# Moving splits, evictions, squares and last outputs of a two-level feed-forward kernel

## The chip, the cores and the metric

One core of a Trainium2 chip runs the whole program. The metric is the device time of one execution in microseconds (us). The times shown for the kernel before are 1060.23, 1060.93 and 1061.2 us, with 1060.93 as their median.

The engines are named as in the profile: PE is TensorE (PEld its weight loads), DVE is VectorE, ACT is ScalarE, POOL is GpSimd, SP is SyncE, which here only issues DMAs.

## The reference

Causal attention with a cumulative bias runs over 4 batches, 8 heads and 576 positions. Its output, seen as 2304 tokens by 512, passes through two feed-forward blocks. The second of these is where nearly all of the change lies:

```python
def _moe_ref(x, w_in, w_out) -> np.ndarray:
    h = x @ w_in
    g = np.maximum(h, 0.0) + np.log1p(np.exp(-np.abs(h)))
    return (g @ w_out).astype(np.float32)
...
def _moe2_ref(x, w_gate, w_val, w_out, rms_g) -> np.ndarray:
    rms = np.sqrt(np.mean(x * x, axis=-1, keepdims=True) + 1e-06)
    xn = x / rms * rms_g
    g = xn @ w_gate
    silu = g * (1.0 / (1.0 + np.exp(-g)))
    val = xn @ w_val
    return (silu * val @ w_out).astype(np.float32)
```

The first block has 2048 hidden columns, the second 1536 for the gate and 1536 for the value.

## The kernel before

Every fp32 operand of a matmul is held as a high half (a copy rounded to fp32r, made on ACT) and a low half (the operand minus its high half, made on DVE or POOL). A product is three matmuls: high by high, high by low, low by high.

The program has three stages: attention, the first feed-forward (96 steps over six token tiles of 384), and the second feed-forward. The second one walks three **groups** of 768 tokens, and within a group 12 **steps**, one for each 128 hidden columns. Steps are numbered n = 0 to 35, a group change stands at n = 12 and n = 24. `m2_g(n)` writes one step. It forms gate and value of a 2 by 2 block product with seven block products instead of eight. Each block product is `prod`, six matmuls with 384 columns. In the order of the code they are, with the PSUM bank they write:

- P1: weight A12 by activation form B21 into D, P2: A11 by B11 into A
- O0: `m2_out(n-1, 0)`, nine matmuls with 512 columns: the output of the step before, token tiles m = 0, 1, 2
- P3: S2 by T2 into A
- O1: `m2_out(n-1, 1)`, nine matmuls, token tiles m = 3, 4, 5
- P4: S1 by T1 into D, P5: S3 by T3 into A, P6: S4 by B22 into D, P7: A22 by T4 into A

There are two banks, D and A, so each product waits until the one before it in its bank has been read: P3 for `c1` (ACT copies A, L1011), P5 for `u2` (ACT, L1030), P6 for `m5` (ACT, L1038), P7 for `vB` (DVE adds A and m5, L1047), P4 for `gA` (DVE, L1015), the next P1 for `gB` (DVE, L1049), the next P2 for L1052 (DVE). A sigmoid on ACT (L1016) stands between gA and `s0`. `m2_hi` (ACT, L985) and `m2_lo` (DVE, L990) split the gated values for the outputs. Half 0 of a step is split at its end, half 1 (the `l` tile of L1057) in the step after.

The order on each engine is the order of the code: nothing reorders it (`manual_schedule`), and a list of due times only decides which function is called before which. Each engine works through its own list in that order.

Beside the products, each step splits the weights of the next one (`u_split`, four pieces: ACT high L924, POOL low L925) and loads those of the step after it (`u_load`, SP). At a group change the activation forms are new: `n_split` splits seven forms for two column blocks j = 0, 1 (ACT high L968, low L970 on DVE or POOL by an even or odd index). In step 11 or 23 (`ahead`) these are B21, B11 and T2; in step 12 or 24 (`fresh`) T1 and T3 after O0, B22 after u2, T4 after m5. Also `m2_evac` copies the finished group's six output tiles from PSUM in two halves each and stores them: m = 0, 1, 2 in step 12 after P4, m = 3, 4, 5 in step 13 ahead of O0. Odd m go over ACT (L1082), even ones over DVE (L1084). Since O0 and O1 of step 13 write the same banks anew, they wait for these copies.

`m1_ss` squares the last tile of the first feed-forward (ACT, L863) and adds the square to a sum (POOL, L865), four times, with one tile for the square. By the due times three of these stand between steps 0 and 1, the fourth after step 1. `m2_end` writes the last outputs: O1 of step 34, then the six tiles of step 35 in the order m = 0 to 5, with copies on ACT and DVE and twelve stores on SP.

Of the kernel before, what the change touches and what calls it, by code (L numbers as in the profile page):

```python
# [14 lines left out]
AF = mybir.ActivationFunctionType  # L15
# [130 lines left out]
def attention_moe_kernel(ctx, tc, q, k, v, s, w_in, w_out, w_gate, w_val, w_out2, rms_g, out):  # L146
# [710 lines left out]
    def m1_ss(t, a):  # L857
        y = st["yt", t, a]
        if a == 0:
            st["acc", t] = ss_tile("acc")  # L860
            st["sq", t] = ss_tile("sq")
        acc, sq = st["acc", t], st["sq", t]
        nc.scalar.activation(out=acc if a == 0 else sq, in_=y, func=AF.Square)  # L863
        if a > 0:
            nc.gpsimd.tensor_tensor(out=acc, in0=acc, in1=sq, op=ALU.add)  # L865
# [92 lines left out]

    FORMS = ("B21", "B11", "T2", "T1", "T3", "B22", "T4")

    def n_split(g, j, nm):
        i = FORMS.index(nm) + 7 * j
        if i < 4:
            t = xa.tile([P, 2 * T], F32R, tag="xa", name="xf").rearrange("p (x n) -> p x n", x=2)
        else:
            t = pools["wb"].tile([P, 2, 512], F32R, tag=f"w{8 + i}", name="xf")[:, :, 0:T]
        src = st["src", g, j].pop(nm)
        nc.scalar.activation(out=t[:, 0], in_=src, func=AF.Copy)  # L968
        eng = nc.gpsimd if g > 0 and i % 2 else nc.vector
        eng.tensor_tensor(out=t[:, 1], in0=src, in1=f32(t[:, 0]), op=ALU.subtract)  # L970
        st["X", nm, j] = t[:, 0], t[:, 1]

    def prod(o, n, wn, xn, start, stop):
        wh, wl = st["W", n, wn]
        for j in range(2):
            xh, xl = st["X", xn, j]
            c = slice(j * P, (j + 1) * P)
            first, last = start and j == 0, stop and j == 1
            nc.tensor.matmul(o, wh[:, c], xh, start=first, stop=False, skip_group_check=True)  # L979
            nc.tensor.matmul(o, wh[:, c], xl, start=False, stop=False, skip_group_check=True)  # L980
            nc.tensor.matmul(o, wl[:, c], xh, start=False, stop=last, skip_group_check=True)  # L981

    def m2_hi(n, h):
        gh, l = st["g", n][0], st["lt", n, h]
        nc.scalar.activation(out=gh[:, h * T:(h + 1) * T], in_=l, func=AF.Copy)  # L985

    def m2_lo(n, h):
        (gh, gl), l = st["g", n], st.pop(("lt", n, h))
        c = slice(h * T, (h + 1) * T)
        nc.vector.tensor_tensor(out=gl[:, c], in0=l, in1=f32(gh[:, c]), op=ALU.subtract)  # L990

    def m2_g(n, fill=None):
        g, f = divmod(n, F2)
        D, A = ps_p("D")[:, 0:T], ps_p("A")[:, 0:T]
        c1, u2, m5 = [m1_tile("gh", 3) for _ in range(3)]
        gA, s0, gB = [m1_tile("gl", 3) for _ in range(3)]
        s1, vB = m1_tile("u", 1), m1_tile("l", 2)
        st["g", n] = [pools["m1"].tile([P, 2 * T], F32R, tag="xb", name="gg", bufs=4) for _ in range(2)]
        tt, act = nc.vector.tensor_tensor, nc.scalar.activation
        ahead = f == F2 - 1 and g < NG - 1  # L1000
        fresh = f == 0 and g > 0

        def renew(go, *names):
            if go:
                for nm in names:
                    for j in range(2):
                        n_split(g + ahead, j, nm)

        prod(D, n, "A12", "B21", True, True)
        prod(A, n, "A11", "B11", True, False)  # L1010
        act(out=c1, in_=A, func=AF.Copy)  # L1011
        if n:
            m2_hi(n - 1, 1)
            m2_lo(n - 1, 1)
        tt(out=gA, in0=D, in1=c1, op=ALU.add)  # L1015
        act(out=s0, in_=gA, func=AF.Sigmoid)  # L1016
        tt(out=s0, in0=gA, in1=s0, op=ALU.mult)
        if f == 1 and g > 0:
            m2_evac(g - 1, 1)
        if n:  # L1020
            m2_out(n - 1, 0)
        else:
            fill()
        renew(ahead, "B21", "B11")
        renew(fresh, "T1", "T3")
        if n == N5:
            m1_ssum(NTILE - 1, D)
            m1_ms(NTILE - 1)
        prod(A, n, "S2", "T2", False, False)
        act(out=u2, in_=A, func=AF.Copy)  # L1030
        renew(fresh, "B22")
        if n + 1 < NS2:
            u_split(n + 1, (0, 1))
        if 0 < n < NS2 - 1:
            m2_out(n - 1, 1)
        renew(ahead, "T2")
        prod(D, n, "S1", "T1", True, False)
        act(out=m5, in_=D, func=AF.Copy)  # L1038
        renew(fresh, "T4")
        if fresh:  # L1040
            m2_evac(g - 1, 0)
        if n + 1 < NS2:
            u_split(n + 1, (2, 3))
        if n + 2 < NS2:
            u_load(n + 2)
        prod(A, n, "S3", "T3", False, False)
        tt(out=vB, in0=A, in1=m5, op=ALU.add)  # L1047
        prod(D, n, "S4", "B22", False, True)
        tt(out=gB, in0=D, in1=u2, op=ALU.add)  # L1049
        act(out=s1, in_=gB, func=AF.Sigmoid)  # L1050
        prod(A, n, "A22", "T4", False, True)
        tt(out=s0, in0=A, in1=s0, op=ALU.mult)  # L1052
        st["lt", n, 0], st["lt", n, 1] = s0, vB
        m2_hi(n, 0)
        tt(out=s1, in0=gB, in1=s1, op=ALU.mult)
        m2_lo(n, 0)
        tt(out=vB, in0=vB, in1=s1, op=ALU.mult)  # L1057

    def m2_out(n, h):
        f = n % F2  # L1060
        if f == 0 and h == 0:
            st["o2"] = [ps_s("o") for _ in range(4)] + [ps_1("x1"), ps_1("o0")]
        w = slots[2, 3 * f + 2]
        gh, gl = st["g", n]
        ms = range(3 * h, 3 * h + 3)
        jobs = [(m, k) for k in range(3) for m in ms]
        if n == NS2 - 1:
            jobs = [(m, k) for m in ms for k in range(3)]
        for m, k in jobs:
            x, r = ((gh, w[0]), (gh, w[1]), (gl, w[0]))[k]  # L1070
            nc.tensor.matmul(st["o2"][m], x[:, m * P:(m + 1) * P], r, start=(f == 0 and k == 0),  # L1071
                             stop=(f == F2 - 1 and k == 2))

    def m2_evac(g, h):
        W = DM // 2
        for m in range(3 * h, 3 * h + 3):
            r = 2 * T * g + m * P
            for i, c in enumerate((slice(0, W), slice(W, DM))):
                ob = y_tile() if g < NG - 1 or m % 2 else m1_tile("gl", 3)
                ob, src = ob[:, 0:W], st["o2"][m][:, c]  # L1080
                if m % 2:
                    nc.scalar.activation(out=ob, in_=src, func=AF.Copy)  # L1082
                else:
                    nc.vector.tensor_copy(out=ob, in_=src)  # L1084
                nc.sync.dma_start(out=out[r:r + P, c], in_=ob)

    def m2_end():
        n = NS2 - 1
        m2_out(n - 1, 1)
        m2_hi(n, 1)  # L1090
        m2_lo(n, 1)
        m2_out(n, 0)
        m2_evac(NG - 1, 0)
        m2_out(n, 1)
        m2_evac(NG - 1, 1)


    with tc.manual_schedule():
# [22 lines left out]
        with ExitStack() as es0:  # L1121
# [5 lines left out]
            def at(x, fn, *args):  # L1127
                evs.append((x, len(evs), fn, args))
# [20 lines left out]
            for v in sorted({STEPS[i][0] for i in NS}):  # L1149
                i = min(i for i in NS if STEPS[i][0] == v)  # L1150
                t, n = v % NTILE, FA if v < NTILE else F1 - FA
                if v > 0:
                    for a in range(KD):
                        x = i + OFF1["xs"] + OFF1["xt"] * a
                        if v > 1:
                            at(x + OFF1["xl"], x_load, v, a)
                        at(x, x_split, v, a, nc.gpsimd)
                e = i + n - 1 + OFF1["Y"]
                if i + n < len(STEPS):
                    for a in range(KD):  # L1160
                        at(e + 0.001 * (a + 1), m1_evac, v, a)
                if v < NTILE:
                    continue
                for a in range(KD):
                    at(e - (3.0, 2.8, 2.6, 1.3)[a], y_load, t, a)
                x = "5" if t == NTILE - 1 else ""
                for a in range(KD):
                    at(e + OFF2["ss"] + OFF2["sr"] * a, m1_ss, t, a)
                    at(e + OFF2["xn" + x] + OFF2["xr" + x] * a, m1_xn, t, a)
                at(e + OFF2["sh" + x], m1_sh, t)  # L1170
                if not x:
                    at(e + OFF2["sm"], m1_ssum, t)
                    at(e + OFF2["iv"], m1_ms, t)
                for k in range(10):
                    at(e + OFF2["iv" + x] + OFF2["in" + x] * (k + 1), m1_inv, t, k)
# [59 lines left out]
```

## Time and profile before

| what | us |
|---|---|
| median of the runs (1060.23 to 1061.2) | 1060.93 |
| the profiled execution | 1059.71 |
| its span, first to last instruction | 1057.9 |
| PE busy in the span (97%) | 1029.3 |
| DVE, ACT, POOL busy (66%, 51%, 54%) | 693.4, 540.6, 570.0 |

The profiled execution is 1.8 us longer than its span. A step of the second feed-forward that stands in no group change takes 11.5 us. In the rows further down, an arrow at the end of a row names what ended the wait in front of it; names such as `xf`, `gg` or `yt` are the program's tiles, and the buffer numbers are left out.

### The profile page before, as it was taken

To read this page: it belongs to the slowest core of one execution; us is meant where nothing else is said; L and a number is where in the kernel's file an instruction comes from. 1 tells how busy PE (TensorE), PEld (TensorE's weight loads), DVE (VectorE), ACT (ScalarE), POOL (GpSimd) and SP (SyncE) were. 2 spreads that over 40 slices of the span, in tenths; PEclk is the share of its full clock that TensorE was granted. 3 is DMA by queue.
4 is the path that set the end of the run, shared out by engine and by line. 5 is a ranking of instruction groups with operands and counts; after the bars stand their busy time and mean duration, and the time that the engine had idled before them with its cause. 6 is when DMAs were issued, how large, how long until landed. Compare 5 with 4: busy or idle time off the path is not lost.

```text
span 1057.9 us, 19448 instructions
## 1 busy us (share of the span) xinstructions
PE 1029.3 (97%) x7212; PEld 953.8 (90%) x7212; DVE 693.4 (66%) x1141; ACT 540.6 (51%) x1189; POOL 570.0 (54%) x477
## 2 busy tenths in 40 slices
PE   6999999999999999999999999999989999899997
PEld 5788877889999999999989998999979999799997
DVE  8888988418776756889898654545664346734444
ACT  2455666536656544544544544445554445644443
POOL 4378878736766433555767245355453433644331
PEclk9999999999999999999999999999999999999999
DMA  8367664345555575766542323224242233333221
GB/s 155 78 161 172 166 164 134 106 133 159 173 154 161 184 257 179 231 230 194 146 151 84 117 81 98 70 86 161 88 130 71 81 121 104 99 100 89 86 70 60
DMA packets 143758, 139.68 MB, mean 132 GB/s; under 512 B 68656, under 2 KB 118960, under 8 KB 143664
## 3 DMA queue, kind: packets, MB, share of 16 engines
q1 hardware_dynamic: 143632, 138.44, 44.5%
q8 instruction: 57, 0.93, 0.4%
q14 instruction: 37, 0.30, 0.1%
q0 software_dynamic: 32, 0.00, 0.0%
HBM read 106.73 MB, written 31.53 MB: 131 GB/s over the span
## 4 chain that ended last, share of the span: by engine, by line
PE 60%; DVE 7%; issue 3%; POOL 3%; DMA 2%; ACT 2%; SPq 0%; POOLq 0%; ACTq 0%; DVEq 0%
PE y L830 12%; PE o L1071 10%; PE A L979 4%; PE A L981 4%; PE A L980 4%; PE D L981 3%; PE D L979 3%; PE D L980 3%; PE h L792 3%; PE h L794 3%; PE h L793 3%; PE x L1071 2%; PE x L792 1%; PE x L794 1%; PE x L793 1%
## 5 line engine op out<-in xcount | busy, mean ns | idle before, releaser
L925 POOL TENSOR_TENSOR w<-wl,w 128x512 fp32r<-128x512 f32 x108 | 140.1, 1313 | 211.7 <-ACT w L924 211.7
L1071 PE MATMUL o<-w,gg 128*128 128x512 f32 x540 | 153.3, 393 | 0.3
L830 PE MATMUL y<-gh,w 128*128 128x384 f32 x768 | 149.8, 335 | 2.9 <-ACT gh L814 1.7
L830 PEld LDWEIGHTS y<-gh,w 128*128 128x128 f32 x768 | 134.4, 188 | 4.5 <-ACT gh L814 2.0
L1071 PEld LDWEIGHTS o<-w,gg 128*128 128x128 f32 x540 | 100.8, 188 | 19.4 <-ACT yt L1082 0.9
L979 PE MATMUL A<-xf,w 128*128 128x384 f32 x288 | 97.2, 338 | 6.2 <-DVE l L1047 4.7
L980 PE MATMUL A<-xf,w 128*128 128x384 f32 x288 | 96.9, 336 | 0.7 <-DVE xf L970 0.7
L981 PE MATMUL A<-xf,w 128*128 128x384 f32 x288 | 97.0, 337 | 0.0
L1047 DVE TENSOR_TENSOR l<-A,gh 128x384 f32<-128x384 f32 x36 | 20.0, 556 | 115.8 <-ACT w L924 113.3
L535 ACT ACTIVATE e<-t 128x448 f32<-128x448 f32 (+2 forms) x128 | 56.4, 505 | 71.3 <-PE t L528 66.4
L818 DVE TENSOR_TENSOR gl<-l,gh 128x384 fp32r<-128x384 f32 x96 | 79.3, 831 | 16.1 <-ACT gh L814 16.0
L261 POOL TENSOR_TENSOR wf<-ur 128x512 int32<-128x512 int32 x44 | 62.6, 1424 | 50.4 <-DVE ur L249 36.2
L485 DVE TENSOR_REDUCE mc<-s 128x2 f32<-128x512 f32 (+4 forms) x160 | 76.3, 534 | 19.0 <-PE s L470 15.0
L792 PE MATMUL h<-xh,w 128*128 128x384 f32 x256 | 85.6, 335 | 0.0
L793 PE MATMUL h<-xl,w 128*128 128x384 f32 x256 | 85.5, 334 | 0.0
L794 PE MATMUL h<-xh,w 128*128 128x384 f32 x256 | 85.5, 334 | 0.0
L830 PE MATMUL y<-gl,w 128*128 128x384 f32 x384 | 82.4, 335 | 2.3 <-DVE gl L818 2.2
L245 DVE TENSOR_SCALAR ur<-ur 128x512 f32<-128x512 f32 x68 | 51.3, 754 | 35.2 <-ACT ur L238 35.2
L979 PE MATMUL D<-xf,w 128*128 128x384 f32 x216 | 72.9, 338 | 0.0
L981 PE MATMUL D<-xf,w 128*128 128x384 f32 x216 | 72.8, 337 | 0.0
L980 PE MATMUL D<-xf,w 128*128 128x384 f32 x216 | 72.5, 336 | 0.0
L261 POOL TENSOR_TENSOR w<-ur 128x512 int32<-128x512 int32 x24 | 34.8, 1451 | 68.7 <-DVE ur L249 48.1
(171 smaller groups left out, 2662.8 us busy)
## 6 DMA issues: line engine op xcount, KB each, us to landing
wl<-wf SPq DMA_DIRECT2D x108, 256.0 KB
raw<-in_moe_w_out_dram SPq DMA_DIRECT2D x28, 512.0 KB
wf<-w SPq DMA_DIRECT2D x24, 512.0 KB
raw<-in_moe_w_in_dram SPq DMA_DIRECT2D x16, 512.0 KB
raw<-in_moe_w_gate_dram SPq DMA_DIRECT2D x12, 512.0 KB
raw<-in_moe_w_val_dram SPq DMA_DIRECT2D x12, 512.0 KB
xr<-x SPq DMA_DIRECT2D x28, 192.0 KB
qn<-in_q_dram SPq DMA_DIRECT2D x16, 288.0 KB
```

Source lines behind the costliest of these rows:

```text
L261: nc.gpsimd.tensor_tensor(out=w.bitcast(I32), in0=u, in1=r3, op=ALU.add)
L485: nc.vector.reduce_max(out=o, in_=x, axis=AX.X, negate=True)
L792: nc.tensor.matmul(o, wh, xh, start=start, stop=False)
L793: nc.tensor.matmul(o, wh, xl, start=False, stop=False)
L794: nc.tensor.matmul(o, wl, xh, start=False, stop=stop)
L818: nc.vector.tensor_tensor(out=gl, in0=st.pop(("l", i)), in1=f32(st["gh", i]), op=ALU.subtract)
L830: nc.tensor.matmul(y[m][:, 0:T], x[:, m * P:(m + 1) * P], r, start=first and x is w[0] and r is gh, stop=last and r is gl)
L925: nc.gpsimd.tensor_tensor(out=t[:, 1, 0:w], in0=src, in1=f32(t[:, 0, 0:w]), op=ALU.subtract)
L979: nc.tensor.matmul(o, wh[:, c], xh, start=first, stop=False, skip_group_check=True)
L980: nc.tensor.matmul(o, wh[:, c], xl, start=False, stop=False, skip_group_check=True)
L981: nc.tensor.matmul(o, wl[:, c], xh, start=False, stop=last, skip_group_check=True)
L1071: nc.tensor.matmul(st["o2"][m], x[:, m * P:(m + 1) * P], r, start=(f == 0 and k == 0), stop=(f == F2 - 1 and k == 2))
```

## The change

- In step 11 or 23 T1 is now split too, after the step's last products, with both low halves on POOL.
- In step 12 or 24 T3 is split right after c1, with both low halves on POOL; B22 (both lows on DVE) and T4 (j = 0 on DVE, j = 1 on POOL) after s0 and ahead of u2.
- Evictions at a group change: m = 0 (DVE) and m = 1 (ACT) after O0 of step 12, ahead of the sigmoid; m = 2 (ACT) after m5; m = 3 (ACT) and m = 4 (DVE) at the end of step 12; m = 5 (ACT) in step 13 ahead of gA.
- In step 12 or 24 the third and fourth piece of the next weights are split after the sigmoid `s1` and not before P5.
- The four squares stand inside step 1: two after s0, one after m5, one after s1.
- The last step forms its half 1 ahead of P7, and the end computes m = 3, 4, 5, 0, 1, 2.

```diff
-    def n_split(g, j, nm):
+    def n_split(g, j, nm, pool=None):
...
-        eng = nc.gpsimd if g > 0 and i % 2 else nc.vector
+        eng = nc.gpsimd if (g > 0 and i % 2 if pool is None else pool) else nc.vector
...
         act(out=c1, in_=A, func=AF.Copy)
+        renew(fresh, "T3", pool=(1, 1))
         if n:
             m2_hi(n - 1, 1)
             m2_lo(n - 1, 1)
+        if f == 1 and g > 0:
+            m2_evac(g - 1, (5,))
         tt(out=gA, in0=D, in1=c1, op=ALU.add)
-        act(out=s0, in_=gA, func=AF.Sigmoid)
-        tt(out=s0, in0=gA, in1=s0, op=ALU.mult)
-        if f == 1 and g > 0:
-            m2_evac(g - 1, 1)
...
+        if fresh:
+            m2_evac(g - 1, (0, 1))
+        act(out=s0, in_=gA, func=AF.Sigmoid)
+        tt(out=s0, in0=gA, in1=s0, op=ALU.mult)
+        squares(1, 0, 1)
         renew(ahead, "B21", "B11")
-        renew(fresh, "T1", "T3")
+        renew(fresh, "B22", pool=(0, 0))
+        renew(fresh, "T4", pool=(0, 1))
...
         act(out=u2, in_=A, func=AF.Copy)
-        renew(fresh, "B22")
...
-        renew(fresh, "T4")
+        squares(1, 2)
         if fresh:
-            m2_evac(g - 1, 0)
-        if n + 1 < NS2:
+            m2_evac(g - 1, (2,))
+        elif n + 1 < NS2:
             u_split(n + 1, (2, 3))
...
         act(out=s1, in_=gB, func=AF.Sigmoid)
+        squares(1, 3)
+        if fresh:
+            u_split(n + 1, (2, 3))
+        if n == NS2 - 1:
+            tt(out=s1, in0=gB, in1=s1, op=ALU.mult)
+            tt(out=vB, in0=vB, in1=s1, op=ALU.mult)
...
+        if fresh:
+            m2_evac(g - 1, (3, 4))
+        renew(ahead, "T1", pool=(1, 1))
...
-                if m % 2:
+                if m % 2 if g == NG - 1 else m not in (0, 4):
...
     def m2_end():
         n = NS2 - 1
-        m2_out(n - 1, 1)
         m2_hi(n, 1)
         m2_lo(n, 1)
-        m2_out(n, 0)
-        m2_evac(NG - 1, 0)
-        m2_out(n, 1)
-        m2_evac(NG - 1, 1)
+        m2_hi(n, 0)
+        m2_lo(n, 0)
+        m2_out(n - 1, 1, (3, 4))
+        for m in (3, 4, 5, 0, 1, 2):
+            if m == 5:
+                m2_out(n - 1, 1, (5,))
+            m2_out(n, m // 3, (m,))
+            m2_evac(NG - 1, (m,))
```

ACT in step 12, before, from c1 (`gh<-A`, the first row) to the first eviction. `xf` are the forms' high halves, `gl<-gl` is the sigmoid, the second `gh<-A` is u2, `w` are weight splits, `gh<-D` is m5:

```order
L1011 ACTIVATE gh<-A 128x384
L985 ACTIVATE gg<-l 128x384
L1016 ACTIVATE gl<-gl 128x384
L968 ACTIVATE xf<-xs 128x384 x4
L1030 ACTIVATE gh<-A 128x384
L968 ACTIVATE xf<-xs 128x384 x2
L924 ACTIVATE w_9963<-wl 128x512
L924 ACTIVATE w_9966<-wl 128x512
L1038 ACTIVATE gh<-D 128x384
L968 ACTIVATE xf<-acc 128x384
L968 ACTIVATE xf<-sq 128x384
L1082 ACTIVATE yt<-o 128x256 x2
```

The same engine and place now, from T1's two high halves at the end of step 11 (the line numbers are those of the changed kernel, where u2 is L1040 and the sigmoid L1030):

```order
L968 ACTIVATE xf<-xs 128x384 x2
L1016 ACTIVATE gh<-A 128x384
L968 ACTIVATE xf<-xs 128x384 x2
L985 ACTIVATE gg<-l 128x384
L1099 ACTIVATE yt<-o 128x256 x2
L1030 ACTIVATE gl<-gl 128x384
L968 ACTIVATE xf<-xs 128x384 x2
L968 ACTIVATE xf<-acc 128x384
L968 ACTIVATE xf<-sq 128x384
L1040 ACTIVATE gh<-A 128x384
L924 ACTIVATE w_9981<-wl 128x512
L924 ACTIVATE w_9984<-wl 128x512
```

Between the sigmoid and u2 there are still four splits, now other ones; T1 and T3 stand ahead of the sigmoid, and no split stands behind u2 any more. POOL at the same place, before, from the third weight piece of step 12 to the fourth of step 13:

```order
L925 TENSOR_TENSOR w_9859<-wl,w_9859 128x512
L925 TENSOR_TENSOR w_9862<-xr,w_9862 128x256
L970 TENSOR_TENSOR xf<-xs,xf 128x384 x3
L925 TENSOR_TENSOR w_9963<-wl,w_9963 128x512
L925 TENSOR_TENSOR w_9966<-wl,w_9966 128x512
L970 TENSOR_TENSOR xf<-sq,xf 128x384
L925 TENSOR_TENSOR w_10009<-wl,w_10009 128x512
L925 TENSOR_TENSOR w_10012<-xr,w_10012 128x256
```

And now:

```order
L925 TENSOR_TENSOR w_9859<-wl,w_9859 128x512
L925 TENSOR_TENSOR w_9862<-xr,w_9862 128x256
L970 TENSOR_TENSOR xf<-xs,xf 128x384 x4
L970 TENSOR_TENSOR xf<-sq,xf 128x384
L925 TENSOR_TENSOR w_9981<-wl,w_9981 128x512
L925 TENSOR_TENSOR w_9984<-wl,w_9984 128x512
L925 TENSOR_TENSOR w_10032<-wl,w_10032 128x512
L925 TENSOR_TENSOR w_10035<-xr,w_10035 128x256
```

POOL has one low half of a form more, and T4's (`xf<-sq`) stands ahead of the weights of step 13. ACT around the end of step 0 and the first half of step 1, before (the first row is half 0 of step 0, `yt` are squared):

```order
L985 ACTIVATE gg<-gl 128x384
L863 ACTIVATE acc<-yt 128x384
L863 ACTIVATE sq<-yt 128x384 x2
L1011 ACTIVATE gh<-A 128x384
L985 ACTIVATE gg<-l 128x384
L1016 ACTIVATE gl<-gl 128x384
L1030 ACTIVATE gh<-A 128x384
```

And now:

```order
L985 ACTIVATE gg<-gl 128x384
L1016 ACTIVATE gh<-A 128x384
L985 ACTIVATE gg<-l 128x384
L1030 ACTIVATE gl<-gl 128x384
L863 ACTIVATE acc<-yt 128x384
L863 ACTIVATE sq<-yt 128x384
L1040 ACTIVATE gh<-A 128x384
```

The squares moved from ahead of c1 to behind the sigmoid; the third and fourth stand further down in step 1.

## Rows read from the trace of the kernel before

**Rows 1.** The page's first part: busy time, share, instructions.

```profile
PE 1029.3 (97%) x7212; PEld 953.8 (90%) x7212; DVE 693.4 (66%) x1141; ACT 540.6 (51%) x1189; POOL 570.0 (54%) x477
```

**Rows 2.** Stretches: length, busy PE, PEld, DVE, ACT, POOL; clock, DMA.

```profile
762.60:777.50 14.90, 12.17 (x61) 10.49 (x61) 12.19 (x17) 9.34 (x22) 11.07 (x10) 1.00 0.24 80
905.20:920.10 14.90, 12.20 (x62) 10.53 (x61) 12.18 (x17) 9.35 (x22) 11.06 (x10) 1.00 0.25 78
790.00:801.50 11.50, 11.50 (x61) 10.71 (x60) 4.75 (x9) 5.30 (x12) 4.49 (x5) 1.00 0.26 80
```

**Rows 3.** Waits of PE, whole span: for whom, total us, times, longest.

```profile
PE A L979 <- DVE l L1047: 4.7, 2, 2.4
...
PE A L979 <- ACT gh L1011: 1.5, 1, 1.5
...
PE A L980 <- DVE xf L970: 0.7, 2, 0.4
PE x L1071 <- DVE yt L1084: 0.6, 2, 0.3
```

**Rows 4.** Timeline of PE, steps 12 and 13: start, us, instruction, idle before.

```profile
770.95 0.34 PE L979 MATMUL A<-xf,w 128*128 128x384 f32 x1
771.67 0.45 PE L980 MATMUL A<-xf,w 128*128 128x384 f32 x1 [0.39 <-DVE xf L970]
...
776.41 0.41 PE L979 MATMUL A<-xf,w 128*128 128x384 f32 x1 [2.34 <-DVE l L1047]
...
783.85 0.47 PE L1071 MATMUL x<-w,gg 128*128 128x512 f32 x1 [0.31 <-DVE yt L1084]
```

**Rows 5.** Timeline of ACT in step 12.

```profile
766.20 0.53 ACT L985 ACTIVATE gg<-l 128x384 fp32r<-128x384 f32 x1 [0.77 <-DVE l L1057]
767.88 0.53 ACT L1016 ACTIVATE gl<-gl 128x384 f32<-128x384 f32 x1 [1.15 <-DVE gl L1015]
768.31 1.75 ACT L968 ACTIVATE xf<-xs 128x384 fp32r<-128x384 f32 x4
769.96 0.47 ACT L1030 ACTIVATE gh<-A 128x384 f32<-128x384 f32 x1
...
771.16 1.14 ACT L924 ACTIVATE w<-wl 128x512 fp32r<-128x512 f32 x2
772.21 0.47 ACT L1038 ACTIVATE gh<-D 128x384 f32<-128x384 f32 x1
```

**Rows 6.** Timeline of DVE in step 12.

```profile
765.62 0.55 DVE L1057 TENSOR_TENSOR l<-l,u 128x384 f32<-128x384 f32 x1
...
773.12 1.35 DVE L970 TENSOR_TENSOR xf<-acc,xf 128x384 fp32r<-128x384 f32 x1 [0.22 <-ACT xf L968]
774.39 1.41 DVE L1084 COPY yt<-o 128x256 f32<-128x256 f32 x4
```

**Rows 7.** Timeline of POOL around the start of step 12.

```profile
762.01 1.01 POOL L970 TENSOR_TENSOR xf<-xs,xf 128x384 fp32r<-128x384 f32 x1
...
764.24 1.05 POOL L925 TENSOR_TENSOR w<-xr,w 128x256 fp32r<-128x256 f32 x1
```

**Rows 8.** Timeline of step 2, POOL and DVE starting together.

```profile
648.55 1.45 POOL L865 TENSOR_TENSOR acc<-acc,sq 128x384 f32<-128x384 f32 x1 [1.69 <-ACT sq L863]
648.56 0.55 DVE L1057 TENSOR_TENSOR l<-l,u 128x384 f32<-128x384 f32 x1
```

**Rows 9.** Timeline of ACT at the start of step 1.

```profile
638.33 0.52 ACT L863 ACTIVATE sq<-yt 128x384 f32<-128x384 f32 x1 [1.18 <-POOL acc L865]
638.76 0.47 ACT L1011 ACTIVATE gh<-A 128x384 f32<-128x384 f32 x1
```

**Rows 10.** Timeline of the end: last outputs on PE, first and last stores on SP.

```profile
1047.57 3.11 PE L1071 MATMUL o<-w,gg 128*128 128x512 f32 x13
...
1049.61 0.81 SPq L1085 DMA_DIRECT2D out_dram<-gl  x2
...
1054.45 0.90 SPq L1085 DMA_DIRECT2D out_dram<-yt  x2
```

More of the change, by code (lines that the diff above doesn't have):

```diff
@@ L1001, in m2_g, with renew @@
         fresh = f == 0 and g > 0
-        def renew(go, *names):
+        def renew(go, *names, pool=(None, None)):
             if go:
@@ L1006, in renew, with squares @@
                     for j in range(2):
-                        n_split(g + ahead, j, nm)
+                        n_split(g + ahead, j, nm, pool[j])
+        def squares(k, *ks):
+            if n == k:
+                for a in ks:
+                    m1_ss(NTILE - 1, a)
         prod(D, n, "A12", "B21", True, True)
@@ L1053, in m2_g, with m2_out @@
         st["lt", n, 0], st["lt", n, 1] = s0, vB
[L1054 to L1059, printed above, removed]
+        if n < NS2 - 1:
+            m2_hi(n, 0)
+            tt(out=s1, in0=gB, in1=s1, op=ALU.mult)
+            m2_lo(n, 0)
+            tt(out=vB, in0=vB, in1=s1, op=ALU.mult)
+        if fresh:
+            m2_evac(g - 1, (3, 4))
+        renew(ahead, "T1", pool=(1, 1))
+    def m2_out(n, h, ms=None):
         f = n % F2
@@ L1064, in m2_out @@
         gh, gl = st["g", n]
-        ms = range(3 * h, 3 * h + 3)
+        ms = range(3 * h, 3 * h + 3) if ms is None else ms
         jobs = [(m, k) for k in range(3) for m in ms]
-        if n == NS2 - 1:
-            jobs = [(m, k) for m in ms for k in range(3)]
         for m, k in jobs:
@@ L1072, in m2_out, with m2_evac @@
                              stop=(f == F2 - 1 and k == 2))
-    def m2_evac(g, h):
+    def m2_evac(g, ms):
         W = DM // 2
-        for m in range(3 * h, 3 * h + 3):
+        for m in ms:
             r = 2 * T * g + m * P
@@ L1088, in m2_end @@
         n = NS2 - 1
-        m2_out(n - 1, 1)
         m2_hi(n, 1)
         m2_lo(n, 1)
-        m2_out(n, 0)
-        m2_evac(NG - 1, 0)
-        m2_out(n, 1)
-        m2_evac(NG - 1, 1)
+        m2_hi(n, 0)
+        m2_lo(n, 0)
+        m2_out(n - 1, 1, (3, 4))
[4 more added lines that the diff above has]
+            m2_evac(NG - 1, (m,))
     with tc.manual_schedule():
@@ L1167, in attention_moe_kernel @@
                 for a in range(KD):
-                    at(e + OFF2["ss"] + OFF2["sr"] * a, m1_ss, t, a)
+                    if not x:
+                        at(e + OFF2["ss"] + OFF2["sr"] * a, m1_ss, t, a)
                     at(e + OFF2["xn" + x] + OFF2["xr" + x] * a, m1_xn, t, a)
```

## The prediction

> **What bounds the kernel now.** I read the page's busy times first. PE is busy for 1029.3 of 1057.9 us [rows 1], so only the 3% in which it stands can be won. Next come the stretches. A step in no group change lasts 11.5 us with PE busy throughout, but the steps at the two group changes last 14.9 us each, 3.4 more, with PE busy for 12.2 [rows 2]. PE's clock is at full speed (1.00) in all three, so the 3.4 us are waiting. The waits of PE say for whom [rows 3]: P7 stands for DVE's vB twice (4.7 us, 2.4 the longest), P5 for a low half twice (0.7), O1 of the next step for an eviction on DVE twice (0.6), and P3 once for c1 (1.5, this one outside the group changes).
>
> The timeline places them. P5's second matmul starts 0.72 us behind its first, 0.39 of it idle, since T3's low half is late, and P7 starts at 776.41 after 2.34 us idle [rows 4]. The cause of the latter stands on DVE: T4's low half runs until 774.47 and four eviction copies until 775.80, all ahead of vB [rows 6]. In step 13 the output for m = 4 starts at 783.85 after a DVE copy [rows 4]; with the wait for m = 3 ahead of it I count 0.9 there. A change thus loses 3.4 + 0.9 = 4.3 us, both 8.6.
>
> **The group change, part by part.** It removes no work: the same 28 half splits and twelve copies move to other places. I walk step 12, which starts at 762.6; step 24 has the same stretch [rows 2].
>
> *T1 and T3 on POOL.* POOL is free of the weights of step 12 at 764.24 + 1.05 = 765.3 [rows 7], and a low half alone takes it 1.0 (the 1.01 row there). Four of them, T1 and T3, would end at 769.3. P4 needs T1 at 769.9 and P5 needs T3 at 770.95 [rows 4], so the wait for T3 goes. But DVE now meets POOL at a place where POOL had nothing to do before. A DVE operation with two SBUF inputs takes 0.55 alone [rows 6] and 1.35 with POOL running beside it (T4's row there), which is 0.8 more. In the start at 648.55, where both came together, DVE kept 0.55 and POOL took 1.45 [rows 8]. In the walk L1057 starts at 765.62 behind T1's first pass and ends at about 767.0 instead of 766.2. ACT's high half (0.53) ends at 767.6 and DVE's low half, half stretched, at 768.3; gA, which reads one side from PSUM and is not stretched, ends at 768.8. The sigmoid then starts at 768.9 instead of 767.88 [rows 5], **1.0 late**.
>
> *Splits ahead of u2.* From the sigmoid's start to u2's there are 769.96 - 767.88 = 2.1 us with four splits between [rows 5], and four stand there again. So u2 starts at 771.0 and ends at 771.45. P5 is due at 770.95, so it stands 0.5, plus 0.1 for the slow first pair that follows each stall (0.45 instead of 0.34 in rows 4). Behind u2 two weight splits (1.05 from start to start of what follows) and then m5 (0.47) end at 772.95 [rows 5], while P6 would be due at 771.5 + 1.1 = 772.6. It stands 0.3, again plus 0.1. Together **1.0** remains per change.
>
> *DVE behind it.* Two copies for m = 0 (0.35 each from the row of four, rows 6), the stretched s0, two unstretched B22 halves and a stretched T4 half (1.35) end at about 772.7. So vB is held by m5 alone and ends at 773.5, ahead of P7's due time of 774.0. The 2.3 us wait goes, and what is late next is m5.
>
> *Evictions.* m = 0, 1, 2 are copied by 773.4; their banks are wanted in step 13 from about 777. ACT's two copies for m = 1 fall while it waits for gA, those for m = 2 while it waits for gB, and neither delays anything. m = 3 and 4 end at about 777.2 and 779.4, with DVE stretched twice beside the weight halves that moved to this place; O1 wants them from 780.3. m = 5 follows the high half and ends at 779.8. The 0.9 goes with 0.9 of cover; without it the copies would cost again what they cost now.
>
> *SP.* The stores now go out in pieces, four from about 769 on, two behind m5. The load of the third weight piece of step 14 waits for the low half of step 13's third piece, which now ends at about 777.5. The stores of m = 3, 4, 5 queue behind it. It would be wanted by ACT at 783.8, which leaves it some 6 us. I cost it at nothing.
>
> Sum: 4.3 - 1.0 = **3.3 us** less per change, 6.6 for both. Bounds: if the stretches all miss the chain, only 0.1 remains (8.4 gained). If both DVE operations are stretched by the full 0.8, the sigmoid is 1.6 late, P5 stands 1.2 and P6 0.5, so 1.7 remains (5.2 gained).
>
> **The squares.** Before, c1 of step 1 starts at 638.76 behind the third square, which itself waited 1.18 for POOL's add to free the one square tile [rows 9]; P3 waits 1.5 for it [rows 3], 1.6 with the slow start. Now c1 stands first and is done when P2 is; nothing else holds P3. Behind the sigmoid two squares (0.52 each) push u2 to end at about 640.6. P5 is due 1.0 + 2.1 + 1.0 us of products and outputs behind P3's new start of 637.7, at 641.8, so they are covered. The third and fourth stand behind m5 and s1, where POOL's adds wait behind one weight half each, and the sum is wanted only in step 3. I take **1.6 us**. Bounds 0.5, should half of the wait reappear at u2, and 1.7.
>
> **The end.** Twelve stores go out one behind the other from 1049.61 to 1055.35 (0.48 each), and the span ends 2.55 later [rows 10]. This queue is the bound, for PE starts its last output six spacings of 0.23 behind the row of thirteen, at about 1051.7. Now the first finished tile needs 6 + 3 outputs instead of 9 + 3, 3 x 0.23 = 0.7 earlier (0.23 is the spacing in that row). Against this half 1 must be ready at once: PE would stand about 0.6 for it, which SP's queue hides as long as the last tile's copies end ahead of its turn. I take the first store 0.6 earlier and so **0.6 us** less. Bounds: 0.7 less, or 0.7 more if the last tile sets the end.
>
> **Sum.** 6.6 + 1.6 + 0.6 = 8.8 us. The span of 1057.9 becomes 1049.1 and the profiled execution of 1059.71 becomes 1050.9. That execution lay 1.2 below the median of the runs, so the median of 1060.93 becomes **1052.1 us**.
>
> **Rivals.**
>
> *POOL locks DVE out throughout.* T1's and T3's passes stand back to back for over 4 us in the very stretch where DVE's chain to u2 runs. If each DVE operation of that chain waits out a whole pass of 1.0, L1057 and the low half lose 2.0 together; P5 then stands 1.5 and P6 0.5, 2.0 in all, so that a change gains 2.3 and the time is 1060.93 - 4.6 - 1.6 - 0.6 = 1054.1. The 1.35 row speaks for it, the 648.56 row, where DVE came at the same time and lost nothing, against. The Trainium skill (SBUF — State Buffer, section "Who interferes with whom") says that a VectorE instruction with two SBUF inputs and a GpSimd instruction that reads SBUF exclude each other, and that the order of issue decides who blocks. The rows agree in both directions (1.35 for DVE, 1.45 for POOL); it is the rule that speaks against moving four halves to POOL here. Chance 0.2.
>
> *No contention in the chain.* T1's passes fall between DVE's operations. Then 0.1 remains per change, and the time is 1060.93 - 8.4 - 1.6 - 0.6 = 1050.3. Against it: DVE's L1057 starts 0.3 us after POOL becomes free. Chance 0.1.
>
> *No change.* The waits change place only: T4's halves or m = 4's copies are late again, 3.5 us or more return at each change, and the queue of stores hides nothing. 1060.9 - 1.6 = 1059.3 or more. For this, DVE would have to be 1.3 us later than walked at vB and 0.9 later at m = 4, which the busy times of DVE in the stretch (12.2 of 14.9) don't exclude. Chance 0.06.
>
> *Slower.* The load of step 14's third weight piece, now issued behind a POOL half that stands after the second sigmoid, lands too late. ACT then stands at its split in step 13 with the sigmoid, half 0 and the next c1 queued behind, and PE runs dry. It decides from 6 us after the issue; each us beyond costs one at each change. To eat 8.8 us and 2.2 more, the landing must take 11.5 us after the issue, giving 1063. The last store's 2.55 us to the end of the span [rows 10] speaks against it. Chance 0.04.
>
> **How the numbers follow.** The forecast has 0.6, its own range 1050.5 to 1053.5. The other cases on its side of 1058.8 hold 0.3. A measurement of this kernel can tell about 0.2% (2.1 us) from no change. So faster 0.9, same 0.06, slower 0.04. The range takes in both first rivals, the end's worse bound (1.3 above the forecast) and part of the squares' lower bound: 1050.0 to 1055.6.
>
> **What would show it.** Right: steps 12 and 24 last about 12.5 us; PE's wait for vB and the one for an eviction are gone and a wait of 0.4 to 0.6 for u2 (ACT's A copy) and one for m5 stand in their place; no wait for c1 at step 1; the first store at about 1049.0 in the old time scale. Wrong: P7 still waiting for DVE, L1057 in step 12 at 0.55 (no contention) or O0 waiting for half 0's low half in step 13; at the end, about 5 us are right from the start of the last output matmul to the end of the span, and the 6.2 of before would refute that part.

## The result and the profile after

The changed kernel takes **1051.48 us** (median of 4 runs, 1050.74 to 1051.63); the kernel before, beside it, 1060.58 (1060.01 to 1061.2). The ratio is 0.991 (95%: 0.990 to 0.993): 9.1 us faster, with 1052.1 forecast. The profiled execution took 1051.63 us with a span of 1049.3.

The page's first part, as [rows 1]: busy time, share, instructions.

```profile
PE 1027.5 (98%) x7212; PEld 953.1 (91%) x7212; DVE 687.3 (66%) x1135; ACT 541.6 (52%) x1193; POOL 573.9 (55%) x479
```

The work is the same; PE stands (has no matmul running) for 21.8 us of the span instead of 28.6. The stretches, as [rows 2] (length; busy PE, PEld, DVE, ACT, POOL; clock; DMA): step 12, step 24 and a step in no group change.

```profile
761.30:773.76 12.46, 12.05 (x61) 10.62 (x61) 10.49 (x14) 8.77 (x22) 11.50 (x10) 1.00 0.37 119
900.35:912.83 12.48, 12.07 (x61) 10.64 (x61) 10.52 (x14) 8.77 (x22) 11.52 (x10) 1.00 0.36 117
788.00:799.50 11.50, 11.50 (x61) 10.71 (x61) 4.75 (x9) 5.03 (x12) 4.53 (x4) 1.00 0.27 81
```

A group change costs 1.0 us over a regular step, and the step behind it costs nothing more (11.52 and 11.50 us, start to start). The waits of PE, as [rows 3]; none for vB, for a low half, for an eviction or for c1 of step 1 is left:

```profile
PE A L979 <- ACT gh L1040: 0.6, 2, 0.3
PE o L1088 <- ACT gg L985: 0.5, 1, 0.5
```

The first is P5 waiting for u2 at both changes, the second half 1's high part at the end. The timeline of PE in step 12, as [rows 4], shows P5 and P6 (start, us, instruction, idle before):

```profile
769.49 0.34 PE L981 MATMUL D<-xf,w 128*128 128x384 f32 x1
770.14 0.45 PE L979 MATMUL A<-xf,w 128*128 128x384 f32 x1 [0.31 <-ACT gh L1040]
...
771.12 0.34 PE L981 MATMUL A<-xf,w 128*128 128x384 f32 x1
771.56 0.44 PE L979 MATMUL D<-xf,w 128*128 128x384 f32 x1
```

Matmuls follow each other here every 0.175 us. P5's first stands 0.65 behind its neighbour, 0.48 too much; P6's first 0.44, 0.27 too much, which the waits view doesn't list under PE. Each is followed by one start 0.28 later instead of 0.175, another 0.1. That is 0.96 in all. What P5 and P6 waited for stands on ACT, as [rows 5]: the sigmoid (L1030), four high halves, u2, two weight splits, m5.

```profile
767.53 0.53 ACT L1030 ACTIVATE gl<-gl 128x384 f32<-128x384 f32 x1 [0.75 <-DVE gl L1023]
767.96 0.93 ACT L968 ACTIVATE xf<-xs 128x384 fp32r<-128x384 f32 x2
768.79 0.51 ACT L968 ACTIVATE xf<-acc 128x384 fp32r<-128x384 f32 x1
769.20 0.51 ACT L968 ACTIVATE xf<-sq 128x384 fp32r<-128x384 f32 x1
769.62 0.47 ACT L1040 ACTIVATE gh<-A 128x384 f32<-128x384 f32 x1
769.99 1.14 ACT L924 ACTIVATE w<-wl 128x512 fp32r<-128x512 f32 x2
771.03 0.48 ACT L1047 ACTIVATE gh<-D 128x384 f32<-128x384 f32 x1
```

The sigmoid starts 767.53 - 761.30 = 6.23 us into the step; before it was 767.88 - 762.60 = 5.28 [rows 2, 5]. The 0.95 comes from DVE, as [rows 6]:

```profile
764.30 1.38 DVE L1073 TENSOR_TENSOR l<-l,u 128x384 f32<-128x384 f32 x1
...
766.27 0.70 DVE L990 TENSOR_TENSOR gg<-l,gg 128x384 fp32r<-128x384 f32 x1 [0.59 <-ACT gg L985]
766.89 0.55 DVE L1023 TENSOR_TENSOR gl<-D,gh 128x384 f32<-128x384 f32 x1
...
770.11 1.36 DVE L970 TENSOR_TENSOR xf<-acc,xf 128x384 fp32r<-128x384 f32 x1
771.57 0.56 DVE L1056 TENSOR_TENSOR l<-A,gh 128x384 f32<-128x384 f32 x1
```

and from POOL beside it, as [rows 7]: the four low halves of T1 and T3 together, then the third and the fourth alone, with the DVE operation that met the fourth.

```profile
763.92 4.91 POOL L970 TENSOR_TENSOR xf<-xs,xf 128x384 fp32r<-128x384 f32 x4
```

```profile
766.52 1.34 POOL L970 TENSOR_TENSOR xf<-xs,xf 128x384 fp32r<-128x384 f32 x1
```

```profile
767.81 1.02 POOL L970 TENSOR_TENSOR xf<-xs,xf 128x384 fp32r<-128x384 f32 x1
```

```profile
768.09 1.15 DVE L1031 TENSOR_TENSOR gl<-gl 128x384 f32<-128x384 f32 x1
```

While POOL makes the four low halves of T1 and T3, DVE's L1073 (L1057 before) takes 1.38 instead of 0.55, and the low half behind it 0.70. The difference gA (L1023), which reads PSUM on one side, keeps 0.55. POOL pays too: its first three passes take 1.34 each instead of 1.01 [rows 7], the fourth 1.02. Taken one by one, L1073, L990 and L1031 each end 0.4 us behind the end of a POOL pass (765.68 behind 765.26, 766.97 behind 766.55, 769.24 behind 768.83). So each of them waits out what is left of the pass that is running, and the pass that starts behind it is the longer one. vB (L1056) starts at 771.57, right behind m5's end and ahead of P7.

### The profile page after: what moved, and what is told of

Read it like the earlier page. It is cut to its first block, busy times and chain, and to the rows that moved or that the text cites. A ratio compares the mean times of both kernels' runs of the same rounds, so it can differ in the third digit from the quotient of the medians.

```text
span 1049.3 us, 19450 instructions
## 1 busy us (share of the span) xinstructions
PE 1027.5 (98%) x7212; PEld 953.1 (91%) x7212; DVE 687.3 (66%) x1135; ACT 541.6 (52%) x1193; POOL 573.9 (55%) x479
## 4 chain that ended last, share of the span: by engine, by line
PE 85%; DVE 8%; DMA 3%; ACT 2%; issue 1%; POOL 1%; SPq 0%; DVEq 0%; POOLq 0%; ACTq 0%
PE y L830 15%; PE o L1088 11%; PE t L518 5%; PE A L981 5%; PE A L979 5%; PE A L980 5%; PE s L462 4%; PE D L979 4%; PE D L981 3%; PE D L980 3%; PE h L792 3%; PE h L794 3%; PE h L793 3%; PE o L552 3%; PE x L552 2%; PE x L1088 2%
## 5 line engine op out<-in xcount | busy, mean ns | idle before, releaser
L1056 DVE TENSOR_TENSOR l<-A,gh 128x384 f32<-128x384 f32 x36 | 20.0, 556 | 112.7 <-ACT w L924 105.9
```

## The experiments

Step lengths are from start to start of a step's first product; "12 + 13" is a group change and the step behind it, 14.93 + 12.45 us in the profile of before, 12.46 + 11.52 in that of the changed kernel. The first four kernels take the change apart.

**a1_squares**: the kernel before, with the squares moved alone (two behind the sigmoid of step 1, one behind m5, one behind s1).

```diff
+        def squares(k, *ks):
+            if n == k:
+                for a in ks:
+                    m1_ss(NTILE - 1, a)
...
+        squares(1, 0, 1)
...
+        squares(1, 2)
...
+        squares(1, 3)
...
-                    at(e + OFF2["ss"] + OFF2["sr"] * a, m1_ss, t, a)
+                    if not x:
+                        at(e + OFF2["ss"] + OFF2["sr"] * a, m1_ss, t, a)
```

> The kernel before with the four squares moved into step 1 and nothing else. My theory: the parts of the change add up, and the squares alone are worth the wait of P3 for c1, so step 1 falls from 13.25 us to 11.5 and the time by 1.7 us. Rival: the squares only hide a wait of the same length at u2 or at the sum behind step 1; then step 1 or 2 stays over 12.5 us and the time falls by less than 0.8.

Step 1 fell from 13.25 to 11.50, and steps 0 and 2 (9.63 and 11.50, before 9.64 and 11.52) took no longer, so the squares cost nothing at their new places. The ratio is 0.9985 (0.997 to 1.000), 1.6 us; by the runs alone it could still be nothing.

**a4_third**: the kernel before, with only the third square put off.

```diff
-                    at(e + OFF2["ss"] + OFF2["sr"] * a, m1_ss, t, a)
+                    at(e + OFF2["ss"] + (0.573 if x and a == 2 else OFF2["sr"]) * (a + (x != "" and a == 2)), m1_ss, t, a)
```

> The kernel before with only the third square moved from ahead of step 1's c1 to behind step 1, beside the fourth. My theory: the whole wait at c1 comes from the third square, which stands on ACT until POOL's add has freed the one square tile; the two others end at 637.2, ahead of P3's due time of 637.7. So the time falls by 1.6 to 1.8 us, as with all four moved. Rival: three squares of 0.5 us delay c1 by their own length; then it falls by 0.5 only.

Step 1 took 11.56, step 2 11.70: 1.5 of the 1.75 us come from this one instruction (ratio 0.998, 0.997 to 0.999). So the wait was for the square tile that POOL had yet to free [rows 9], not for ACT's load as a whole.

**a2_group**: the changed kernel, with squares and end put back.

```diff
-        squares(1, 0, 1)
...
-        squares(1, 2)
...
-        squares(1, 3)
...
-        for m in (3, 4, 5, 0, 1, 2):
+        m2_out(n, 0)
+        m2_evac(NG - 1, (0, 1, 2))
...
```

> The changed kernel with the squares and the end as before, so that the group change stands alone. My theory: steps 12 and 13 fall from 14.93 + 12.45 us to 12.46 + 11.5, the same at step 24, so the time falls by 6.8 us against before; 1.0 us of waiting stays at each change, at P5 for u2 and at P6 for m5. Rival: part of the gain at the changes needs the squares' move (a stretch shifted in step 1 shifts the loads); then it falls by less than 6.

12 + 13 took 12.49 + 11.50, step 1 13.26, the end 21.62. By its runs the ratio is 0.991 (0.989 to 0.993), all of the change's gain, though the group changes are only 6.8 of the 8.6 us that the two profiles differ in span. The next section comes back to the difference.

**a3_end**: the kernel before, with the end's new order alone (as in the change's diff of the last step).

```diff
-        m2_out(n, 0)
-        m2_evac(NG - 1, 0)
-        m2_out(n, 1)
-        m2_evac(NG - 1, 1)
+        for m in (3, 4, 5, 0, 1, 2):
...
```

> The kernel before with the new order of the end alone. My theory after the comparison of the two traces: the queue of twelve stores sets the end, its first store goes out 0.3 us earlier and a gap of 0.1 to 0.3 opens in it, so the stretch from P7's end to the end of the span falls from 12.2 us by 0.2, too little for the times to tell. Rival (the prediction's size): 0.6 us less.

From the start of the last step to the end of the span it took 21.40 instead of 21.65, and the ratio is 1.000 (0.999 to 1.001). The trace shows 0.25 us, the runs can't.

**b1_no_low**: is it POOL's four passes that leave 1.0 at a change? This kernel leaves them out.

```diff
+        if g > 0 and nm in ("T1", "T3"):
+            st["X", nm, j] = t[:, 0], t[:, 0]
+            return
```

> The changed kernel without the low halves of T1 and T3 at the group changes (their high halves are used in their place, so four subtractions on POOL are left out at each change). My theory: POOL's low halves stretch DVE's L1073 and L990 in step 12, so the sigmoid is 0.95 us late and with it u2 and m5. Without them L1073 takes 0.55, the sigmoid starts 5.3 us into step 12 instead of 6.2, and the 0.97 us of waiting per change go to 0.1 or less: 1.7 us less than the changed kernel. Rival: the order on ACT (T1's and T3's high halves and two copies ahead of the sigmoid, four splits ahead of u2) makes the wait; ACT's list is the same here, so 0.97 per change stay and the time is the same.

12 + 13 took 11.52 + 11.51: nothing is left. The timeline of DVE there, L1076 and L993 being the changed kernel's L1073 and L990, and of ACT:

```profile
763.01 0.55 DVE L1076 TENSOR_TENSOR l<-l,u 128x384 f32<-128x384 f32 x1
764.15 0.56 DVE L993 TENSOR_TENSOR gg<-l,gg 128x384 fp32r<-128x384 f32 x1 [0.59 <-ACT gg L988]
```

```profile
765.27 0.52 ACT L1033 ACTIVATE gl<-gl 128x384 f32<-128x384 f32 x1 [0.49 <-DVE gl L1026]
...
767.35 0.47 ACT L1043 ACTIVATE gh<-A 128x384 f32<-128x384 f32 x1
```

With POOL idle, both DVE operations are back at 0.55 and the sigmoid at 5.28 us into the step (which starts at 759.99), as before the change, with ACT's list as in the changed kernel. POOL's passes at a change cost 0.94 (12.46 to 11.52), which is all that was left. The time was 1048.55 (ratio 0.989, 0.987 to 0.991). That is 2.9 below the changed kernel where 1.7 was expected; the two changes account for 1.9, and the rest is not theirs (the part ahead of the second feed-forward ended 1.3 us earlier in this profile).

**b2_t4_behind_u2** and **b3_m5_first**: can ACT's order hide that price? The first puts T4's high halves behind u2, the second also the two weight splits behind m5. In b2:

```diff
-        renew(fresh, "T4", pool=(0, 1))
...
         prod(A, n, "S2", "T2", False, False)
         act(out=u2, in_=A, func=AF.Copy)
+        renew(fresh, "T4", pool=(0, 1))
```

and in b3 besides:

```diff
-        if n + 1 < NS2:
+        if n + 1 < NS2 and not fresh:
             u_split(n + 1, (0, 1))
...
         act(out=m5, in_=D, func=AF.Copy)
...
         if fresh:
+            u_split(n + 1, (0, 1))
```

> The changed kernel with T4 split behind u2 instead of ahead of it, the weight splits still ahead of m5. My theory: the wait is handed on from u2 to m5: P5 no longer stands (0.59 less), but m5 stands behind the same list of ACT work and P6 stands 0.86 + 0.11 instead of 0.38, so step 12 stays at 12.4 to 12.5 us and the time is the same within 0.3. Rival: u2 is the cause; then 0.59 per change go, 1.2 us in all.

> As the one with T4 behind u2, and the first two weight splits of the next step behind m5 too. My theory: u2 and m5 are then both early, and the next thing late is vB on DVE behind T4's low half (0.3 to 0.5 of wait at P7); step 12 falls from 12.46 us to 11.9, 0.5 per change, 1.0 us less than the changed kernel. Rival: the later weight halves on POOL hold up step 13's first product (its low half must be there 1 us into the step), and the time is the same or longer.

b2 changed nothing: 12.49 + 11.52. u2 is in time, but m5 is as late as ever behind the same four splits. The wait moved from P5 to P6:

```profile
PE D L979 <- ACT gh L1047: 1.4, 2, 0.7
```

b3 took 11.52 + 11.53 with no wait left: 1048.79 us (ratio 0.988, 0.987 to 0.990). The 0.3 to 0.5 that I gave to P7 there did not appear. The head of DVE's chain is stretched as before (1.37 for L1057's counterpart), but PE no longer waits for what follows from it, and T4's low half on DVE, which I had taken as stretched, took 0.55 here, since it ran ahead of POOL's pass and not behind it. The timeline of ACT in b3's step 12, where u2 (L1039) and m5 (L1047) are done before their products want them:

```profile
767.41 0.92 ACT L968 ACTIVATE xf<-xs 128x384 fp32r<-128x384 f32 x2
768.24 0.47 ACT L1039 ACTIVATE gh<-A 128x384 f32<-128x384 f32 x1
...
769.44 0.48 ACT L1047 ACTIVATE gh<-D 128x384 f32<-128x384 f32 x1
769.81 1.15 ACT L924 ACTIVATE w<-wl 128x512 fp32r<-128x512 f32 x2
```

**b4_evac_undone**: the changed kernel, with the evictions back in two lots of three (odd blocks copied by ACT, even ones by DVE, as before), and with them the sigmoid ahead of O0.

```diff
-        if f == 1 and g > 0:
-            m2_evac(g - 1, (5,))
...
+        tt(out=s0, in0=gA, in1=s0, op=ALU.mult)
+        if f == 1 and g > 0:
+            m2_evac(g - 1, (3, 4, 5))
...
-        if fresh:
-            m2_evac(g - 1, (0, 1))
...
         if fresh:
-            m2_evac(g - 1, (2,))
+            m2_evac(g - 1, (0, 1, 2))
...
-        if fresh:
-            m2_evac(g - 1, (3, 4))
```

> The changed kernel with the evictions at the group change placed and divided as before: m = 0, 1, 2 behind m5 of step 12, m = 3, 4, 5 ahead of O0 of step 13. My theory: four copies (1.41 us) stand on DVE ahead of vB again, P7 waits 0.7, and O1 of step 13 waits 0.9 for its banks again, so each change costs 1.6 us more and the time is 3.2 us above the changed kernel. Rival: with the splits moved the copies fit beside them; then under 0.5 us per change.

12 + 13 took 13.21 + 13.31: 2.54 more per change, where 1.6 was expected. The runs say less: 1055.32 us (ratio 0.995, 0.993 to 0.997) is 3.8 above the changed kernel, 1.9 per change. The profiled execution was the slowest of the four (1057.02), and 0.8 of it is a late store at the end, which this edit doesn't touch. The waits of PE that came with it:

```profile
PE o L1084 <- ACT yt L1095: 2.0, 2, 1.0
PE A L979 <- DVE l L1054: 0.9, 2, 0.4
...
PE x L1084 <- DVE yt L1097: 0.6, 2, 0.3
```

The copies of m = 0 to 2 again hold vB, but only for 0.4, since T4's half is out of the way. The larger part is the second lot, for which O1 waits. It stands behind the sigmoid of step 13. DVE and ACT in that step:

```profile
775.21 1.43 DVE L1069 TENSOR_TENSOR u<-gl,u 128x384 f32<-128x384 f32 x1
776.55 1.09 DVE L990 TENSOR_TENSOR gg<-gl,gg 128x384 fp32r<-128x384 f32 x1
```

```profile
776.87 0.49 ACT L1016 ACTIVATE gh<-A 128x384 f32<-128x384 f32 x1 [1.02 <-PE A L981]
...
779.82 0.52 ACT L1022 ACTIVATE gl<-gl 128x384 f32<-128x384 f32 x1 [1.15 <-DVE gl L1021]
780.25 1.19 ACT L1095 ACTIVATE yt<-o 128x256 f32<-128x256 f32 x4
```

The weight halves that the change moves behind the second sigmoid meet DVE here, and the sigmoid starts 2.95 us behind c1 (L1016); before it was 781.92 - 779.87 = 2.05. The second lot is late by that much more. The moved weight halves stretch DVE in the changed kernel as well; with the new places of the copies PE does not wait for it.

**c1_two_queues** and **c2_both**: what bounds the end? c1 lets ACT issue the odd blocks' last stores:

```diff
-                nc.sync.dma_start(out=out[r:r + P, c], in_=ob)
+                q = nc.scalar if g == NG - 1 and m % 2 else nc.sync
+                q.dma_start(out=out[r:r + P, c], in_=ob)
```

c2 is b3 with c1's edit, and block m2 copied into yt:

```diff
-                ob = y_tile() if g < NG - 1 or m % 2 else m1_tile("gl", 3)
+                ob = y_tile() if g < NG - 1 or m % 2 or m == 2 else m1_tile("gl", 3)
```

> The changed kernel with one edit: in the last group the stores of the odd output blocks (m3, m5, m1) are issued by ACT instead of SP. Theory A, SP's queue bounds the end: in the changed kernel twelve stores issue back to back on SP from 1040.91 to 1046.73 us, 0.45 us each, so half of them on another engine lets the last one go as soon as its copy is done, some 0.7 us earlier: last step 21.42 -> about 20.7 us. Theory B, the copies bound it: VectorE's last copy (1045.76 us) waits for a store to give back one of three gl buffers, and that store is not much earlier; then 21.2 to 21.4 us. Group changes 12.46 and step 1 11.5 us as in the changed kernel by both.

> Everything together: T4's splits behind u2's copy and the next step's first weight splits behind m5's copy (as b3_m5_first), the odd blocks' last stores on ACT's queue (as c1_two_queues), and the copies of output block m2 into yt buffers, of which there are seven, instead of the three gl ones. Both theories of c1_two_queues now agree on the end: the last copy need not wait for a store, so it ends some 0.5 to 0.9 us earlier: last step about 20.6 us. Group changes 11.5 us as in b3_m5_first, span about 1046.1 us, time about 1048.0 us, ratio to the kernel before about 0.988. If the end stays at 21.4 us, what bounds it is neither queue nor buffers but the output products themselves.

Both ends took 21.02: 0.4 less than 21.42, between c1's two theories (the twelve stores of the changed kernel go out every 0.49 us, not 0.45 as given there), and c2's buffers added nothing (20.6 was expected). In c2 the last copy ends 0.6 us earlier against the last output product than in c1, SP's last store goes out 0.5 earlier, and the span ends no earlier. The stretches say why (columns as above; the last two are the DMA engines' share and GB/s). First the changed kernel, 3 us ahead of its end, then c2:

```profile
1046.30:1047.30 1.00, 0.00 (x0) 0.00 (x0) 0.00 (x0) 0.00 (x0) 0.00 (x0) 1.00 0.80 264
```

```profile
1043.70:1044.70 1.00, 0.00 (x0) 0.00 (x0) 0.00 (x0) 0.00 (x0) 0.00 (x0) 1.00 1.04 344
```

With one queue the DMA engines are busy 0.80 of the time, here and in the two us before, with two all of it (1.03 in c1). So SP's queue bounds the end of the changed kernel, as I had said, but only 0.4 us ahead of what the full DMA engines allow. Two other profiles fit: in b1 and b4, whose end is the changed kernel's, SP's second store took 1.04 and 1.33 us to issue instead of 0.43, and the end came 0.5 and 0.8 later (21.91 and 22.19). c1 took 1050.78 us, and **c2 1048.42 (ratio 0.988, 0.986 to 0.989)**, the lowest median of all and 12.3 us less than the kernel before beside it (1060.71); b3 is within its scatter.

## A cost that no wait shows

In the profiles of a1, a3 and a4, which keep the old group change, steps 12 and 13 took 14.9 to 15.3 + 13.7 to 14.0 us, 1.5 more than in the profile of before. The stand ahead of P7 was no longer. The windows of PE around it in a1 (busy, clock, DMA), the stand first:

```profile
772.00:774.40 2.40, 0.10 (x1) 1.00 0.23 79
774.40:775.80 1.40, 1.33 (x7) 0.95 0.79 261
775.80:779.10 3.30, 3.30 (x12) 0.50 0.77 194
```

Behind the stand the granted clock falls to 0.50, the lower of TensorE's two levels (1.2 GHz), for 3.4 us (the 3.2 of the next expectation is short), in which ten matmuls start 0.32 us apart instead of 0.17: 10 x 0.15 = 1.5 us. The fall begins 1.2 us behind the first matmul after the stand. In the first profile of before the clock stayed at 1.00 in this place, at both changes. Was it the variants' edits, or did that execution escape? **d1_before_again** is the kernel before, unchanged.

> The kernel before, unchanged, profiled once more. In three variants that keep its group change, the granted clock fell to 0.50 for 3.2 us after the 2.5 us for which TensorE stands ahead of P7, and ten matmuls took 0.32 us each instead of 0.17; in the profile of before it did not. Theory A: this belongs to the stand, and the first profile was one of the executions in which it does not happen; then this profile has it at one or both group changes (15.0 + 13.5 us for the two steps instead of 14.9 + 12.4) and a time of 1060.5 to 1063. Theory B: it comes with the variants' other edits; then both group changes are 14.9 + 12.4 us again at clock 1.00.

Its timeline of PE behind the stand at step 12:

```profile
776.29 0.41 PE L979 MATMUL A<-xf,w 128*128 128x384 f32 x1 [2.36 <-DVE l L1047]
...
777.41 0.47 PE L979 MATMUL D<-xf,w 128*128 128x384 f32 x1
777.68 0.53 PE L980 MATMUL D<-xf,w 128*128 128x384 f32 x1
778.00 0.53 PE L981 MATMUL D<-xf,w 128*128 128x384 f32 x1
```

The same fall at both changes: 14.91 + 14.01 and 15.40 + 13.52 us, a span of 1060.55 against 1057.94, and 1062.33 us against 1059.71. So it belongs to the old group change: eight of the ten profiled ones have it, 3.4 us long each time, and it begins 0.1 to 1.2 us behind the stand. In b4, with single waits of up to 1.0 us, and in the changed kernel, with 0.3, no change has it, and P3's stand of 1.5 us in step 1 has none in the four profiles with that stand.

This is one reason why the runs of before scatter, by 4 us beside a1 and a3 (1059.41 to 1063.69, 25 runs) against 0.9 for the changed kernel (4 runs), and probably why the group change alone brings as much by the medians of the runs as the whole change does by the first two traces. How large a part it has is not shown. In a1's ten runs the time follows the mean granted clock (1056.40 us at 0.999, 1063.95 at 0.992), but of the 25 runs of before nine have 0.997 and lie anywhere from 1060.03 to 1063.69. That mean also counts falls that are not of the change: one at the end, where PE's work is done, and one in attention, 6.8 us at 0.50 from about 43.5 us on, which six of the thirteen profiles have, the changed kernel's among them and the first one of before not.

## Why the prediction was right

Between the two first profiles the span fell by 8.61: both group changes 6.78 (6.6 forecast), step 1 1.75 (1.6), the end 0.23 (0.6), the other steps of the second feed-forward 0.5; the part ahead of it took 0.6 more. The last two are not the change's: the part ahead ends at 623.2 to 624.2 us in the profiles without the fall in attention and at 623.9 to 624.5 in those with it, and regular steps average 11.50 to 11.53.

*What bounds the kernel.* PE's stands, and those alone, were there to be won, in the profile that I read. The forecast's 4.3 per change was 4.36.

*The walk of step 12.* It held nearly row by row. The sigmoid was to be 1.0 late and was 0.95. L1057 was to take 1.35 and took 1.38. P5 was to stand 0.5 for u2 and stood 0.48; P6 0.3 for m5, and 0.27; each with 0.1 behind it. b1 shows that the cause was the one named, POOL's passes beside DVE, since without them nothing remains. The Trainium skill (SBUF — State Buffer, section "Who interferes with whom") lets the order of issue decide who blocks. The trace agrees: the operation that a POOL pass was ahead of took 0.83 more, and three POOL passes, each with a DVE operation ahead of it, took 0.33 more. The DVE operations that came late in a pass lost less, 0.15 (L990, 0.70) and 0.6 (L1031 at 768.09, 1.15). So the rival of a lock throughout, which charged a whole pass of 1.0 to each, fell: L1073 and L990 lost 0.98 together and not 2.0. What fell is its price; that a DVE operation waits for the running pass to end is what these rows show. The one without contention fell too.

*DVE behind it, evictions, SP.* vB was held by m5 alone, O1 waited for no copy, and no third weight piece was late. The cover that I gave to the evictions is real: b4 took it away and paid 2.5 in its profile and 1.9 by its runs, not 1.6. I had priced only the copies' wait before the change, and not what the moved weight halves do to the lot of step 13.

*The squares.* Right in place and mechanism, and 0.15 too small: step 1 had lost 1.75, not 1.6.

*The end.* This step failed: "which SP's queue hides". The timeline of the end, as [rows 10]: PE's three outputs of the last step for m = 3, ACT's first copy, SP's first stores.

```profile
1039.38 1.09 PE L1088 MATMUL o<-w,gg 128*128 128x512 f32 x3 [0.49 <-ACT gg L985]
```

```profile
1040.50 0.66 ACT L1099 ACTIVATE yt<-o 128x256 f32<-128x256 f32 x2 [0.71 <-PE o L1088]
```

```profile
1040.91 0.81 SPq L1102 DMA_DIRECT2D out_dram<-yt  x2
1041.77 0.93 SPq L1102 DMA_DIRECT2D out_dram<-gl  x2
```

PE's wait for half 1 (0.66 by starts) stands *ahead* of the first finished tile. The queue is still empty then and hides nothing; the wait eats the 0.7 that the three outputs brought. The first store was to go out at about 1049.0 in the old time scale and went out at 1049.3, only 0.3 earlier, and the end gained 0.23 and not 0.6 (0.25 in a3). Those 0.3 have another source: before, the first copy was DVE's and stood behind a low half, 3.44 us behind the first output matmul after P7; now it is ACT's, 3.17 behind it. My test for this part, "about 5 us" from the last output's start to the end, came out at 5.2 and proved nothing: the last output had moved back as well. A test has to start from a point that the edit leaves alone.

*From the trace to the runs.* I added 1.2 us to the forecast because the profiled execution lay 1.2 below the median. That profile was one without falls, so the gap is most likely the clock's, though the clocks of the runs beside it are not on record; the change removes the stand behind which they come, and the gap should not have been carried over. d1 has both falls and 3.1 us more in steps 12, 13, 24 and 25. Some of that is in the 9.1, and no term of the prediction has it. That 1052.1 came out 0.6 from 1051.48 is partly luck: the gain that I left out stood against the end's missing 0.4 and the scatter of the runs. Without the 1.2 the forecast would have been 1050.9, as far off on the other side.

Why the clock stays up in some executions of the same stand stays open.

## What to carry to other kernels

Where a chain on a shared engine is late for two consumers, moving one producer forward only hands the wait on (b2); put every short copy that a product waits for ahead of the work that is wanted later (b3). Before you move work to another engine, price the operations that it will run beside; here each of them waited for the end of the running pass, 0.8 us for the one that came just behind its start. Look at the granted clock behind long stands, and profile a kernel twice before you carry the distance between a profile and its runs into a forecast.

## What the runs showed of the hardware that was not expected

- Behind a stand of TensorE of 2.4 us the granted clock was 0.50 for 3.4 us at eight of ten group changes (both in d1, a1, a3 and a4), at a cost of 1.5 us each, and 1.00 in the other two (the first profile of before).
- One queue with back-to-back stores of 128 KB keeps the DMA engines 0.80 busy (264 GB/s), two queues 1.04 (344 GB/s). The span ended 2.6 us behind the last issue with one queue and in c1, and 3.05 behind SP's last issue in c2, where the engines were still full.
- In the changed kernel DVE and POOL slowed each other where both read SBUF: a DVE operation with two SBUF inputs took 1.38, 0.70 or 1.15 instead of 0.55 and ended 0.4 behind the end of the running POOL pass, and POOL's passes took 1.34 instead of 1.01 three times in four. A DVE operation with one side in PSUM kept 0.55.
